# A new order in the attention rounds of a fused attention and expert kernel: query projections behind the keys', ScalarE's copies moved, six early weights split on GpSimd

## Chip, cores and metric

One core of one Trainium2 chip. The metric is device time in microseconds (us), the median of the runs shown; lower is better.

## What is computed

The reference is linear attention with exponential features, and behind it a routed expert layer. Cut to what matters:

```
phi(x):  p = x @ w_phi;  p -= max|p| over the features;  [exp(p), exp(-p)]
kv  = sum over s of phi(k) v          z = sum over s of phi(k)
x   = phi(q) kv / (phi(q) z + 1e-6)   8 batches, 8 heads, 576 tokens, head size 64
e   = argmax(x @ w_gate), or the expert of the token before where local_gate >= 0.5
out = softmax(x @ w_gate)[e] * (relu(x @ w1[e]) @ w2[e])     8 experts, 512 -> 1024 -> 512
```

## The kernel before

**Rounds.** The attention runs in 48 rounds (`round`, line 553) of 384 token positions of a pair of heads, and two more that finish it. Each round works on three generations at once. For its own tokens R it projects the keys into the PSUM tile `pk` and the queries into the PSUM tile `pq` (`proj`, line 326: two banks of 512 columns, two buffers of `pq`), and takes maximum and difference of both on VectorE (`below`, line 335: `mk`, `sbk`, `mq`, `sbq`). For R-1 it turns the query differences into a `pq` tile (`qtr`, line 360), takes their two exponentials on ScalarE (`qexp`, line 366, tile `qp`), and sums keys times values on TensorE (`kv`, `kv4`, tile `kvp`). For an older one it multiplies query features with the summed keys (`num`, line 450) into bank 0 of the tile that held the turned queries; ScalarE copies that to `xo` (line 469) and GpSimd scales it (`scaled`, line 472), sums the gate logits and hands it to a DMA that writes the DRAM array `xs`. There are four buffers of `xo`.

**Summed keys.** When a sum over a batch's keys is complete (two rounds in three), `kv_end` (line 414) copies it to `kvs` on ScalarE (lines 420, 421). The next round turns it: four transposes into columns 384 to 511 of a `pq` tile (line 426), a copy `ks` back on ScalarE (line 433), four small matmuls with the gate weights into the same tile (line 441, "gates"), and a copy of those into `kvs` (line 445). Only then may `num` use `kvs`. Before the change, the four transposes go into the tile of the round before (`past`), into which right behind them the twelve query transposes go (line 572); the queries' projections of the new round follow, into the other buffer.

**What sets the order.** TensorE's order is the order of the code (`manual_schedule`, line 140). The other engines' instructions are placed by a scheduler, held by `issue_after(x)` (not ahead of x on its engine) and `high_priority`. `last_act` and `last_copy` name the last exponential and the last copy on ScalarE. `kv_end` issues its copies behind `last_act`:

```
419  with self.tc.high_priority(), self.tc.issue_after(self.last_act.ins):
420      self.act.copy(kvs[:, :, MID]..., t[:, :, :, 0:D])
421      self.act.copy(kvs[:, :, DEN], t[:, :, :, D])
```

**Background work.** Twice a round `chores` (line 602) takes steps of generators: the routing of a finished batch (`gate`, its reads copied by ScalarE), the scatters of token lists and gathers of tokens by GpSimd's indirect DMAs, each held behind a small copy `tick` (`paced`, line 612), and, when the first two expert slots are planned, the weights of the first of them (`early_weights`, line 523): eight pieces of 128x1024 are loaded into `wraw` (three buffers), and each is split in two halves (`half`, line 544): ScalarE casts to `whi`, GpSimd subtracts to `wlo`.

**Experts.** Behind the rounds the expert slots run (`slots`, line 1408): every product is three float32r matmuls of high and low parts. There ScalarE casts and VectorE subtracts the later weights (`split`, line 1138), one piece at a time as buffers come free. While the first slot runs, the last batch's routing is done on VectorE, with a few small matmuls written into TensorE's order.

Of the kernel before, what the change touches and what calls it, by code (L numbers as in the profile page):

```python
# [7 lines left out]
F32 = mybir.dt.float32  # L8
# [9 lines left out]
B, H, S, D = 8, 8, 576, 64  # L18
# [8 lines left out]
MID, DEN = slice(10, 10 + 2 * D), slice(9, 11 + 2 * D, 2 * D + 1)  # L27
# [4 lines left out]
NR = NBP * NHP * 3  # L32
PLACE = 16
LAG = 1
WE, WR, WL = 8, 3, 2
FILL = 4
ROW = 5
LINE = 256

STEP = "step"  # L40
# [38 lines left out]
class Kernel:  # L79
# [9 lines left out]
    def run(self):  # L89
        nc, tc, A = self.nc, self.tc, self.A  # L90
        act, dve = self.act, self.dve
        with ExitStack() as root:
# [32 lines left out]
            self.tail, self.drained, self.ranked, self.late = False, False, None, 0  # L125
            self.eslots, self.scattered, self.recs = [], [], []
            self.g, self.ch, self.kvb, self.lg, self.kvp, self.summed = {}, {}, {}, {}, {}, {}
            self.f, self.ready, self.scale = {}, {}, []
            self.turns, self.gates, self.background = [], [], []
            self.fetched = 0  # L130
            self.fetch_kq(0)
# [60 lines left out]
            def singles():  # L192
# [4 lines left out]
                       later=[[listed], [no, no, singles] + [lambda k=k: m[k]() for k in (1, 2, 3)] + [more]])  # L197
# [165 lines left out]
            for c in range(3):  # L363
                self.halves(self.f[R]["qt"], (h * 3 + c) * 64, self.f[R]["sq"][:, h, c])

    def qexp(self, R):

        qp = self.f[R]["qp"] = self.feat.tile([128, 2, 2, 384], F32, name="qp")
        src = self.f[R]["qt"][:, :, 0:384].rearrange("p r (a k) -> p a r k", k=64)
        for sg in (0, 1):  # L370
            self.last_copy = self.act.activation(qp[:, sg].rearrange("p h (c r k) -> p (h c) r k", c=3, r=2), src,  # L371
                                                 AF.Exp, scale=1.0 - 2 * sg)

# [40 lines left out]
    def kv_end(self, u, b, t):  # L414


        hp = u % NHP
        kvs = self.back2.tile([128, 2, 2 * (KV + D + 1)], F32, name="kvs", bufs=3)
        with self.tc.high_priority(), self.tc.issue_after(self.last_act.ins):
            self.act.copy(kvs[:, :, MID].rearrange("p s (h d) -> p s h d", h=2), t[:, :, :, 0:D])  # L420
            self.act.copy(kvs[:, :, DEN], t[:, :, :, D])
        e = {}

        def turn(t):
            for sg in (0, 1):
                self.halves(t, 384 + sg * 64, kvs[:, sg, MID])
            self.gates.append(gate)
            return copy

        def copy(t):  # L430
            e["ks"] = self.back2.tile([128, 2, 128], F32, name="ks")
            with self.tc.high_priority():
                self.act.copy(e["ks"].rearrange("p s (r k) -> p s r k", r=2),
                              t[:, :, 384:512].rearrange("p r (s k) -> p s r k", s=2))

        def gate(t):

            g = t[:, 1, 476:512].rearrange("p (s h e) -> p s h e", s=2, h=2)
            for sg in (0, 1):
                for r in (slice(0, 64), slice(64, 128)):  # L440
                    mm = self.last_g = self.pe.matmul(g[r, sg], e["ks"][:, sg, r], self.wgi[:, hp], start=True, stop=True)
                    for x in self.reads:
                        self.tc.declare_no_dep(mm.ins, x.ins, reason="it reads the tile's other bank")
            with self.tc.high_priority(), self.tc.issue_after(self.last_copy.ins):
                self.last_copy = self.act.copy(kvs.rearrange("p s (h x) -> p s h x", h=2)[:, :, :, 0:9], g)  # L445
            self.kvb[u, b] = kvs
            self.ready.update({3 * u + x: 1 for x in ((0,) if b == 0 else (1, 2))})
        self.turns.append(turn)

    def num(self, R, t):  # L450

        u, k = divmod(R, 3)
        bp, hp = divmod(u, NHP)
        c0 = 3 * k
        t = t[:, 0:6 * KV].rearrange("p (c k) -> p c k", c=3)
        qp = self.f[R]["qp"]
        for c in range(3):
            for h in (0, 1):
                k = slice(h * KV, h * KV + KV)
                for sg in (0, 1):  # L460
                    for x in (0, 1):
                        r = slice(64 * x, 64 * x + 64)
                        kvs = self.kvb[u, int(2 * (c0 + c) + x > 8)]
                        self.last_num = self.pe.matmul(t[r, c, k], qp[:, sg, h, c * 128 + 64 * x:c * 128 + 64 * x + 64],  # L464
                                                       kvs[:, sg, k], start=sg == 0, stop=sg == 1)
        del self.f[R]
        xo = self.back2.tile([128, 3, 2 * KV], F32, name="xo", bufs=4)
        with self.tc.high_priority(), self.tc.issue_after(self.last_act.ins):
            self.act.copy(xo, t)
        self.scale.append(lambda: self.scaled(R, bp, hp, c0, xo))  # L470

    def scaled(self, R, bp, hp, c0, xo):
# [35 lines left out]
    def early_chores(self, s, f):  # L508

        w = self.early_weights()  # L510
        for x in f:
            next(w, None)
            yield x
        for x in s:
            for u in range(x["n"]):
                with self.paced():
                    self.gather_x(x, u)
                next(w, None)
                yield STEP
        for _ in w:  # L520
            yield STEP

    def early_weights(self):

        s = self.eslots[0]
        for i in range(min(WE, 8) + LAG):
            if i >= LAG:

                raw, whole = s["raw"].pop(0), self.halved(s)
                self.half(raw, whole, 0)  # L530
            if i < min(WE, 8):
                self.load(s, i)
            yield
            if i >= LAG:
                self.half(raw, whole, 1)
            yield
# [7 lines left out]
    def half(self, raw, whole, k):  # L544

        hi, lo = whole
        c = slice(k * 512, k * 512 + 512)
        with self.tc.issue_after(self.last_act.ins):
            self.act.copy(hi[:, c], raw[:, c])
            for c in (slice(k * 512, k * 512 + 256), slice(k * 512 + 256, k * 512 + 512)):  # L550
                self.pool.tensor_sub(lo[:, c], raw[:, c], hi.bitcast(F32)[:, c])

    def round(self, R):

        new, old = R < NR, 1 <= R <= NR
        if new:
            self.f[R] = {}
            kt = self.psk.tile([128, 2, 512], F32, name="pk")
            self.proj(R, 0, kt)
            sk = self.below(kt, "k")  # L560
        scale, self.scale = self.scale, []
        for x in scale:
            x()
        gates, self.gates = self.gates, []
        turns, self.turns = self.turns, []
        past = self.past_qt if R else None
        copies = [x(past) for x in turns]
        for x in copies:
            x(past)
        gates, self.gates = gates + self.gates, []  # L570
        if old:
            self.qtr(R - 1)
        qt = self.past_qt = self.psq.tile([128, 2, 512], F32, name="pq")
        if new:
            self.f[R]["qt"] = qt
            self.proj(R, 1, qt)
        if old:
            self.qexp(R - 1)
        self.small_ps = [qt[:, 0, 384:512]]
        self.reads = []  # L580
        self.chores()
        mid = 3 * (R - 1) + 1
        if old and mid % NC == 4:
            self.kv4(mid)
        for x in gates:
            x(qt)
        if new:
            self.kexp(R, sk)
            self.f[R]["sq"] = self.below(qt, "q")
        if old:  # L590
            for i in range(3 * (R - 1), 3 * R):
                if i % NC != 4:
                    self.kv(i)
        for k, i in enumerate(sorted(self.ready)[:1 if new else 2]):
            del self.ready[i]
            self.num(i, past[:, 0] if k == 0 else qt[:, 0])
            if not new:
                self.scale.pop()()
        self.small_ps = []
        self.chores()  # L600

    def chores(self):

        for x in list(self.background):
            for _ in range(6):
                y = next(x, self)
                if y is self:
                    self.background.remove(x)
                if y is self or y is STEP:
                    break  # L610
# [958 lines left out]
```

## Time and profile before

| | |
|---|---|
| runs of the kernel | 741.54, 745.0, 744.31 us; median 744.31 |
| the profiled execution | 746.75 us |
| its span, from the first to the last instruction | 744.6 us |
| TensorE busy | 714.7 us, 96% of the span |
| VectorE, ScalarE, GpSimd busy | 421.7, 360.8, 221.5 us |
| granted TensorE clock, mean | 0.994 |

The profile is of one execution; busy time of an engine counts its instructions, not the waits between them. TensorE's weight loads (PEld) run beside its matmuls (PE). A wait is put down to the engine, line and tile that released it last.

### The profile page before, as it was taken

The page shows a single profiled execution, that of the slowest core. Times are in us where ns is not written, and L with a number is a line of the kernel's source. Part 1 is how long each engine was busy: PE and PEld are TensorE (multiplying, and loading weights), DVE is VectorE, ACT ScalarE, POOL GpSimd, SP SyncE. Part 2 cuts the span into 40 slices and gives each one's busy share as a digit, 9 for nine tenths or more (in the row PEclk, how much of TensorE's full clock was granted, in tenths as well). Part 3 has the DMA queues.
Part 4 walks back from the last instruction along what each step waited for, and adds up shares of the span by engine and source line. Part 5 has one row for each costly group of instructions (what it writes and reads, how often), then busy time and mean ns, then how long its engine had stood idle before and what let it go on. Part 6 is the DMA issues. An engine that isn't in the chain of part 4 may idle for free. (4 is left out here: it accounts for less than half of the span.)

```text
span 744.6 us, 22107 instructions
## 1 busy us (share of the span) xinstructions
PE 714.7 (96%) x9448; PEld 623.0 (84%) x9448; DVE 421.7 (57%) x796; ACT 360.8 (48%) x626; POOL 221.5 (30%) x327
## 2 busy tenths in 40 slices
PE   7999999999998989999999999999999999999997
PEld 6888888888888888989888986788878768888985
DVE  6677777677776774584627324544533265453512
ACT  5677767677777866242625224341412055150302
POOL 0322212632377955473232131021212202101011
PEclk9999999999999999999999999999999999999999
DMA  7664454544467761134766984544667364334110
GB/s 228 194 195 131 138 136 130 157 140 130 133 189 217 229 222 38 36 116 132 234 226 198 377 315 149 176 166 155 241 250 282 114 236 170 138 117 160 58 39 29
DMA packets 65540, 125.11 MB, mean 168 GB/s; under 512 B 6908, under 2 KB 44732, under 8 KB 65382
## 3 DMA queue, kind: packets, MB, share of 16 engines
q1 hardware_dynamic: 57152, 100.83, 42.3%
q0 software_dynamic: 7968, 22.58, 8.7%
q8 instruction: 75, 1.23, 0.7%
q10 hardware_dynamic: 320, 0.26, 0.1%
q14 instruction: 25, 0.20, 0.1%
HBM read 102.11 MB, written 21.80 MB: 166 GB/s over the span
## 5 line engine op out<-in xcount | busy, mean ns | idle before, releaser
L1333 ACT ACTIVATE hh<-l 128x512 fp32r<-128x512 f32 (+3 forms) x84 | 44.2, 527 | 196.3 <-PE l L1282 131.7
L1280 PE MATMUL l<-whi,hh 128*128 128x512 f32 (+1 forms) x288 | 114.1, 396 | 0.0
L1334 DVE SCALAR_TENSOR_TENSOR hl<-l,hh 128x512 fp32r<-128x512 f32 (+3 forms) x84 | 50.5, 601 | 112.1 <-ACT hh L1333 111.9
L1150 DVE TENSOR_TENSOR wlo<-wraw,whi 128x1024 fp32r<-128x1024 f32 x80 | 96.5, 1224 | 29.8 <-ACT whi L1147 29.4
L1281 PE MATMUL l<-wlo,hh 128*128 128x512 f32 (+1 forms) x288 | 112.5, 391 | 0.0
L1282 PE MATMUL l<-whi,hl 128*128 128x512 f32 (+1 forms) x288 | 112.4, 390 | 0.0
L1280 PE MATMUL l<-xhi,whi 128*128 128x384 f32 (+4 forms) x308 | 106.8, 347 | 0.0
L1282 PE MATMUL l<-xhi,wlo 128*128 128x384 f32 (+4 forms) x308 | 106.5, 346 | 0.0
L1281 PE MATMUL l<-xlo,whi 128*128 128x384 f32 (+4 forms) x308 | 106.4, 345 | 0.0
L1147 ACT CAST whi<-wraw 128x1024 fp32r<-128x1024 f32 x80 | 81.9, 1046 | 26.9 <-PE l L1282 15.8
L1399 POOL DMA_INDIRECT out<-y,p_tokm x31 | 35.8, 1154 | 190.4 <-DVE y L1393 172.8
L371 ACT ACTIVATE qp<-pq 128x768 f32<-128x768 f32 x96 | 72.6, 808 | 33.3 <-PE pq L358 33.3
L464 PE MATMUL pq<-kvs,qp 128*64 128x74 f32 x2304 | 82.7, 228 | 0.4 <-ACT kvs L445 0.4
L479 POOL TENSOR_TENSOR xo<-xo,rc 128x444 f32<-128x444 f32 x48 | 44.7, 930 | 123.4 <-issue 58.3
L351 ACT ACTIVATE kp<-sbk 128x768 f32<-128x768 f32 x96 | 77.0, 852 | 6.4 <-DVE sbk L342 5.1
L464 PEld LDWEIGHTS pq<-kvs,qp 128*64 128x64 f32 x2304 | 78.1, 137 | 0.5 <-ACT kvs L445 0.5
L386 PE MATMUL kvp<-v,kp 128*64 128x65 f32 x2048 | 72.6, 228 | 0.0
L341 DVE TENSOR_REDUCE mk<-pk 128x6 f32<-128x768 f32 x48 | 45.9, 956 | 46.1 <-PE pk L332 42.1
L386 PEld LDWEIGHTS kvp<-v,kp 128*64 128x64 f32 x2048 | 66.5, 142 | 1.4 <-issue 0.2
L1393 DVE TENSOR_SCALAR y<-l,p_probm 128x512 f32<-128x512 f32 (+1 forms) x31 | 23.2, 749 | 77.0 <-PE l L1282 76.7
L1199 POOL DMA_INDIRECT xg<-xs,p_tokm x32 | 30.9, 965 | 119.3 <-PE tr L1261 101.9
L1282 PEld LDWEIGHTS l<-whi,hl 128*128 128x128 f32 (+1 forms) x288 | 53.2, 185 | 12.4
(266 smaller groups left out, 1189.3 us busy)
## 6 DMA issues: line engine op xcount, KB each, us to landing
wraw<-in_w1h SPq DMA_DIRECT2D x44, 512.0 KB
wraw<-in_w2h SPq DMA_DIRECT2D x44, 512.0 KB
kq<-in_kqT SPq DMA_DIRECT2D x47, 384.0 KB
v<-in_va SPq DMA_DIRECT2D x48, 195.0 KB
xs<-xo SPq DMA_DIRECT2D x48, 192.0 KB
whi<-in_w1h SPq DMA_DIRECT2D x8, 512.0 KB
wlo<-in_w1h SPq DMA_DIRECT2D x8, 512.0 KB
whi<-in_w2h SPq DMA_DIRECT2D x8, 512.0 KB
```

What stands on the lines that cost most here:

```text
L341: dve.tensor_reduce(m, x, AX.X, ALU.max, apply_absolute_value=True)
L351: self.last_act = self.act.activation(kp[:, :, :, sg, :].rearrange("p c h f -> p h c f"), sb, AF.Exp, scale=1.0 - 2 * sg)
L371: self.last_copy = self.act.activation(qp[:, sg].rearrange("p h (c r k) -> p (h c) r k", c=3, r=2), src, AF.Exp, scale=1.0 - 2 * sg)
L386: self.pe.matmul(t[r, sg, h], kp[:, h, sg, r], v[:, h], start=first and sg + h == 0, stop=last and sg + h == 2)
L464: self.last_num = self.pe.matmul(t[r, c, k], qp[:, sg, h, c * 128 + 64 * x:c * 128 + 64 * x + 64], kvs[:, sg, k], start=sg == 0, stop=sg == 1)
L479: pool.tensor_mul(x, x, rc.unsqueeze(3).broadcast_to([128, 3, 2, KV]))
L1147: self.act.copy(hi, raw)
L1150: (low or self.dve).tensor_sub(lo[:, c], raw[:, c], hi.bitcast(F32)[:, c])
L1280: mm(o, ah, bh, start=first, stop=False)
L1281: mm(o, ah, bl, start=False, stop=False)
L1282: self.last_pe = mm(o, al, bh, start=False, stop=last)
L1334: self.marks[dve] = dve.scalar_tensor_tensor(hl[:, hc, m], t, 0.0, hh[:, hc, m].bitcast(F32), ALU.max, ALU.subtract)
```

## The change

Five edits. The queries' projections stand right behind the keys'. The summed keys are turned into the new round's `pq` tile, and only the query transposes go into the round's before, their own. The first query exponential stands ahead of the gates, the second behind their copy. The `kvs` copies are put behind the round's `xo` copy (a list `later`), and `xo` becomes `last_act`. The early weights are six in place of eight, their casts are GpSimd's, and they take a step once a round in place of twice.

```diff
+EW = 6
@@ qexp
-    def qexp(self, R):
+    def qexp(self, R, sg):
+        if sg == 0:
+            self.f[R]["qp"] = self.feat.tile([128, 2, 2, 384], F32, name="qp")
-        for sg in (0, 1):
+        with self.tc.issue_after(self.last_copy.ins) if sg else nullcontext():
             self.last_copy = self.act.activation(...)
@@ kv_end
+        def fetch():
+            with self.tc.high_priority(), self.tc.issue_after(self.last_act.ins):
                 ...
+        if self.past_qt is self.f.get(NR - 1, {}).get("qt") or max(self.f) < NR - 1:
+            self.later.append(fetch)
+        else:
+            fetch()
@@ num
-            self.act.copy(xo, t)
+            self.last_act = self.act.copy(xo, t)
@@ early_chores, early_weights
         for x in f:
-            next(w, None)
+            if not self.second:
+                next(w, None)
...
-        for i in range(min(WE, 8) + LAG):
+        for i in range(EW + LAG):
@@ half
-        with self.tc.issue_after(self.last_act.ins):
-            self.act.copy(hi[:, c], raw[:, c])
-            for c in (slice(k * 512, k * 512 + 256), slice(k * 512 + 256, k * 512 + 512)):
-                self.pool.tensor_sub(lo[:, c], raw[:, c], hi.bitcast(F32)[:, c])
+        self.pool.tensor_copy(hi[:, c], raw[:, c])
+        for c in (slice(k * 512, k * 512 + 256), slice(k * 512 + 256, k * 512 + 512)):
+            self.pool.tensor_sub(lo[:, c], raw[:, c], hi.bitcast(F32)[:, c])
@@ round
+        past = self.past_qt if R else None
+        qt = self.past_qt = self.psq.tile([128, 2, 512], F32, name="pq")
         if new:
             self.proj(R, 0, kt)
             sk = self.below(kt, "k")
...
+        if new:
+            self.proj(R, 1, qt)
-        copies = [x(past) for x in turns]
-        for x in copies:
-            x(past)
+        for x in [x(qt) for x in turns]:
+            x(qt)
         if old:
             self.qtr(R - 1)
-        qt = self.past_qt = self.psq.tile([128, 2, 512], F32, name="pq")
-        if new:
-            self.proj(R, 1, qt)
-        if old:
-            self.qexp(R - 1)
+            self.qexp(R - 1, 0)
...
         for x in gates:
             x(qt)
+        if old:
+            self.qexp(R - 1, 1)
...
+        later, self.later = self.later, []
+        for x in later:
+            x()
-        self.small_ps = []
+        self.small_ps, self.second = [], True
         self.chores()
+        self.second = False
```

TensorE in a turned round, one early in the rounds; before (`pq<-first,kvs` are the turns, `pq<-first,sbq` the query transposes, line 441 the gates, line 464 `num`):

```order
L332 MATMUL pk<-first,kq 128x128 x6
L358 MATMUL pq<-first,kvs 128x64 x4
L358 MATMUL pq<-first,sbq 128x64 x12
L332 MATMUL pq<-first,kq 128x128 x6
L441 MATMUL pq<-wgi,ks 64x18 x4
L386 MATMUL kvp<-v,kp 64x65 x24
L464 MATMUL pq<-kvs,qp 64x74 x24
```

The same round after the change:

```order
L333 MATMUL pk<-first,kq 128x128 x6
L333 MATMUL pq<-first,kq 128x128 x6
L359 MATMUL pq<-first,kvs 128x64 x4
L359 MATMUL pq<-first,sbq 128x64 x12
L450 MATMUL pq<-wgi,ks 64x18 x4
L389 MATMUL kvp<-v,kp 64x65 x24
L473 MATMUL pq<-kvs,qp 64x74 x24
```

The queries' six projections moved ahead of the turns; the query transposes now stand directly ahead of the gates, between the turns and the readers of `ks`.

ScalarE in a turned round, from one `xo` to the last copy ahead of the next; before (the first `kvs` is the gates' copy, the two behind `kp` fetch the next sum):

```order
L469 COPY xo<-pq 128x444
L433 COPY ks<-pq 128x256
L371 ACTIVATE qp<-pq 128x768 x2
L445 COPY kvs<-pq 128x4x9
L351 ACTIVATE kp<-sbk 128x2x3x128 x2
L420 COPY kvs<-kvp 128x2x128
L421 COPY kvs<-kvp 128x2x2
```

After:

```order
L478 COPY xo<-pq 128x444
L425 COPY kvs<-kvp 128x2x128
L426 COPY kvs<-kvp 128x2x2
L442 COPY ks<-pq 128x256
L374 ACTIVATE qp<-pq 128x768
L454 COPY kvs<-pq 128x4x9
L374 ACTIVATE qp<-pq 128x768
L352 ACTIVATE kp<-sbk 128x2x3x128 x2
```

The two fetching copies moved from ahead of `xo` to behind it, and the gates' copy stands between the two exponentials of the queries.

GpSimd where the first early weight is split; before (line 551 subtracts, 479 is the product of `xo`, 811 a scatter):

```order
L618 COPY tick<-mq 128x1
L811 DMA lst<-pr,ri 36992x16
L551 TENSOR_TENSOR wlo<-wraw,whi 128x256 x4
L618 COPY tick<-mk 128x1
L811 DMA lst<-pr,ri 36992x16
L479 TENSOR_TENSOR xo<-xo,rc 128x444
L486 TENSOR_TENSOR lg<-lg,xo 128x27
```

After (line 561 is the cast, 563 subtracts, 488 is the product, 825 a scatter):

```order
L632 COPY tick<-mk 128x1
L825 DMA lst<-pr,ri 36992x16
L561 CAST whi<-wraw 128x512 x2
L488 TENSOR_TENSOR xo<-xo,rc 128x444
L563 TENSOR_TENSOR wlo<-wraw,whi 128x256
L495 TENSOR_TENSOR lg<-lg,xo 128x27
L563 TENSOR_TENSOR wlo<-wraw,whi 128x256
L496 TENSOR_TENSOR lg<-lg,xo 128x27
L563 TENSOR_TENSOR wlo<-wraw,whi 128x256 x2
```

The casts now stand in GpSimd's queue ahead of the product of `xo`, and the subtractions between its sums.

## Rows read from the trace of the kernel before

**Rows 1.** The page, part 1: busy us, share and instructions of each engine

```profile
PE 714.7 (96%) x9448; PEld 623.0 (84%) x9448; DVE 421.7 (57%) x796; ACT 360.8 (48%) x626; POOL 221.5 (30%) x327
```

**Rows 2.** Waits of TensorE and its weight loader: us in total, times, longest

```profile
PE pq L358 <- ACT ks L433: 13.9, 30, 0.5
PE pq L358 <- DVE sbq L342: 1.4, 5, 0.6
...
PEld pq L358 <- ACT ks L433: 18.0, 30, 0.6
```

**Rows 3.** Timeline, a turned round: start, us, engine, line, operation, count [idle before]

```profile
87.40 0.94 PE L332 MATMUL pk<-first,kq 64*128 64x128 f32 x12
87.56 0.53 ACT L469 COPY xo<-pq 128x444 f32<-128x444 f32 x1 [0.37 <-DMA kq<-in_kqT]
...
88.17 0.29 PE L358 MATMUL pq<-first,kvs 64*128 64x64 f32 x4
...
88.49 0.37 ACT L433 COPY ks<-pq 128x256 f32<-128x256 f32 x1 [0.40 <-PE pq L358]
...
88.92 0.59 PE L358 MATMUL pq<-first,sbq 64*128 64x64 f32 x12 [0.46 <-ACT ks L433]
...
89.34 0.89 PE L332 MATMUL pq<-first,kq 64*128 64x128 f32 x12
...
89.54 1.51 ACT L371 ACTIVATE qp<-pq 128x768 f32<-128x768 f32 x2 [0.68 <-PE pq L358]
...
90.16 0.41 PE L441 MATMUL pq<-wgi,ks 128*64 128x18 f32 x8
...
90.41 1.60 PE L386 MATMUL kvp<-v,kp 128*64 128x65 f32 x48
...
91.01 1.60 ACT L351 ACTIVATE kp<-sbk 128x768 f32<-128x768 f32 x2
...
91.84 1.71 PE L464 MATMUL pq<-kvs,qp 128*64 128x74 f32 x48
...
93.48 0.94 PE L332 MATMUL pk<-first,kq 64*128 64x128 f32 x12
```

**Rows 4.** Timeline, the plain round ahead of it

```profile
82.19 0.94 PE L332 MATMUL pk<-first,kq 64*128 64x128 f32 x12
...
82.96 0.53 PE L358 MATMUL pq<-first,sbq 64*128 64x64 f32 x12
...
83.53 1.51 ACT L371 ACTIVATE qp<-pq 128x768 f32<-128x768 f32 x2 [0.65 <-PE pq L358]
...
84.15 0.70 PE L399 MATMUL kvp<-v,kp 64*64 64x65 f32 x32
...
85.75 1.71 PE L464 MATMUL pq<-kvs,qp 128*64 128x74 f32 x48
```

**Rows 5.** Busy time by stretch: PE, PEld, DVE, ACT, POOL, PEclk, DMA, GB/s

```profile
234.00:238.00 4.00, 4.00 (x79) 3.88 (x79) 2.70 (x4) 3.79 (x8) 2.86 (x7) 0.57 0.34 82
```

**Rows 6.** Timeline of TensorE, the two longest waits among the early weights

```profile
232.10 0.34 PE L358 MATMUL pq<-first,kvs 64*128 64x64 f32 x4 [1.01 <-ACT kvs L421]
...
267.26 0.94 PE L332 MATMUL pq<-first,kq 64*128 64x128 f32 x12 [1.38 <-ACT xo L469]
```

**Rows 7.** Groups by line, GpSimd: count | busy us, mean ns | idle before

```profile
L479 POOL TENSOR_TENSOR xo<-xo,rc 128x444 f32<-128x444 f32 x48 | 44.7, 930 | 123.4 <-issue 58.3 <-ACT qp L371 35.8 <-ACT kvs L445 9.5
L811 POOL DMA_INDIRECT lst<-pr,ri x36 | 36.9, 1026 | 14.4 <-DVE ri L75 7.4 <-issue 5.4
...
L551 POOL TENSOR_TENSOR wlo<-wraw,whi 128x256 fp32r<-128x256 f32 x32 | 22.3, 730 | 4.0 <-ACT whi L549 3.9
L486 POOL TENSOR_TENSOR lg<-lg,xo 128x27 f32<-128x27 f32 x36 | 8.7, 242 | 2.8
...
L618 POOL COPY tick<-mq 128x1 f32<-128x1 f32 x21 | 4.0, 191 | 22.5 <-DVE mq L341 22.5
```

**Rows 8.** Groups by line, VectorE: the splits of later weights

```profile
L1150 DVE TENSOR_TENSOR wlo<-wraw,whi 128x1024 fp32r<-128x1024 f32 x80 | 96.5, 1224 | 29.8 <-ACT whi L1147 29.4
```

More of the change, by code (lines that the diff above doesn't have):

```diff
@@ L127, in run @@
             self.g, self.ch, self.kvb, self.lg, self.kvp, self.summed = {}, {}, {}, {}, {}, {}
-            self.f, self.ready, self.scale = {}, {}, []
+            self.f, self.ready, self.scale, self.later, self.second = {}, {}, [], [], False
             self.turns, self.gates, self.background = [], [], []
@@ L364, in qtr @@
                 self.halves(self.f[R]["qt"], (h * 3 + c) * 64, self.f[R]["sq"][:, h, c])
-    def qexp(self, R):
-        qp = self.f[R]["qp"] = self.feat.tile([128, 2, 2, 384], F32, name="qp")
+    def qexp(self, R, sg):
+        if sg == 0:
+            self.f[R]["qp"] = self.feat.tile([128, 2, 2, 384], F32, name="qp")
+        qp = self.f[R]["qp"]
         src = self.f[R]["qt"][:, :, 0:384].rearrange("p r (a k) -> p a r k", k=64)
-        for sg in (0, 1):
+        with self.tc.issue_after(self.last_copy.ins) if sg else nullcontext():
             self.last_copy = self.act.activation(qp[:, sg].rearrange("p h (c r k) -> p (h c) r k", c=3, r=2), src,
@@ L418, in kv_end @@
         kvs = self.back2.tile([128, 2, 2 * (KV + D + 1)], F32, name="kvs", bufs=3)
-        with self.tc.high_priority(), self.tc.issue_after(self.last_act.ins):
-            self.act.copy(kvs[:, :, MID].rearrange("p s (h d) -> p s h d", h=2), t[:, :, :, 0:D])
-            self.act.copy(kvs[:, :, DEN], t[:, :, :, D])
+        def fetch():
+            with self.tc.high_priority(), self.tc.issue_after(self.last_act.ins):
+                self.act.copy(kvs[:, :, MID].rearrange("p s (h d) -> p s h d", h=2), t[:, :, :, 0:D])
+                self.act.copy(kvs[:, :, DEN], t[:, :, :, D])
+        if self.past_qt is self.f.get(NR - 1, {}).get("qt") or max(self.f) < NR - 1:
+            self.later.append(fetch)
+        else:
+            fetch()
         e = {}
@@ L517, in early_chores @@
                     self.gather_x(x, u)
-                next(w, None)
+                if not self.second:
+                    next(w, None)
                 yield STEP
@@ L521, in early_chores @@
             yield STEP
+            while self.second:
+                yield STEP
     def early_weights(self):
         s = self.eslots[0]
-        for i in range(min(WE, 8) + LAG):
+        for i in range(EW + LAG):
             if i >= LAG:
@@ L530, in early_weights @@
                 self.half(raw, whole, 0)
-            if i < min(WE, 8):
+            if i < EW:
                 self.load(s, i)
@@ L547, in half @@
         c = slice(k * 512, k * 512 + 512)
-        with self.tc.issue_after(self.last_act.ins):
-            self.act.copy(hi[:, c], raw[:, c])
-            for c in (slice(k * 512, k * 512 + 256), slice(k * 512 + 256, k * 512 + 512)):
-                self.pool.tensor_sub(lo[:, c], raw[:, c], hi.bitcast(F32)[:, c])
+        self.pool.tensor_copy(hi[:, c], raw[:, c])
+        for c in (slice(k * 512, k * 512 + 256), slice(k * 512 + 256, k * 512 + 512)):
+            self.pool.tensor_sub(lo[:, c], raw[:, c], hi.bitcast(F32)[:, c])
     def round(self, R):
         new, old = R < NR, 1 <= R <= NR
+        past = self.past_qt if R else None
+        qt = self.past_qt = self.psq.tile([128, 2, 512], F32, name="pq")
         if new:
-            self.f[R] = {}
+            self.f[R] = {"qt": qt}
             kt = self.psk.tile([128, 2, 512], F32, name="pk")
@@ L563, in round @@
             x()
-        gates, self.gates = self.gates, []
+        if new:
+            self.proj(R, 1, qt)
         turns, self.turns = self.turns, []
-        past = self.past_qt if R else None
-        copies = [x(past) for x in turns]
-        for x in copies:
-            x(past)
-        gates, self.gates = gates + self.gates, []
+        for x in [x(qt) for x in turns]:
+            x(qt)
         if old:
             self.qtr(R - 1)
-        qt = self.past_qt = self.psq.tile([128, 2, 512], F32, name="pq")
-        if new:
-            self.f[R]["qt"] = qt
-            self.proj(R, 1, qt)
-        if old:
-            self.qexp(R - 1)
+            self.qexp(R - 1, 0)
         self.small_ps = [qt[:, 0, 384:512]]
@@ L584, in round @@
             self.kv4(mid)
+        gates, self.gates = self.gates, []
         for x in gates:
             x(qt)
+        if old:
+            self.qexp(R - 1, 1)
         if new:
```

## The prediction

> **What bounds the kernel now.** I read the page's busy shares first. TensorE is busy 714.7 of 744.6 us [rows 1]: what an edit can win is either TensorE's 30 us of idle time, or time in which TensorE works slowly. The waits of TensorE say where the idle time is: 30 times, 0.46 us each, the transposes of the queries (line 358) wait for ScalarE's copy `ks` [rows 2]. The weight loader shows the same wait as 18.0 us, 0.60 each, since its work can't run ahead either. All this lies in the 48 rounds before 302 us; behind them TensorE shows no wait worth naming, so a gain there is kept to the end.
>
> Then one round of each kind on the timeline. In a *turned* round [rows 3] (summed keys are turned: two rounds in three) the reader is to see 6.08 us from one `pk` to the next (87.40 to 93.48), and in it 0.75 us between the four turns (88.17) and the queries' transposes (88.92), which is ScalarE's copy there and back. A *plain* round [rows 4] takes 5.21 us (82.19 to 87.40) and has no such hole. Last, the stretch in which the early weights are split: TensorE stands still 1.01 us for `kvs` and 1.38 us for `xo` [rows 6], both behind a cast of weights in ScalarE's queue, and some us after each the granted clock is 0.57 over 4 us (one of the two stretches stands in [rows 5]; the other, 268 to 272, reads 0.57 as well), so partly at the lower of its levels, 1.2 of 2.4 GHz.
>
> **The turned round, step by step.** All offsets are from the start of `pk`. Before: turns +0.77, copy `ks` +1.09 to +1.46, queries' transposes +1.52, `pq` +1.94, gates +2.76, `kvp` +3.01, `num` +4.44, end +6.08 [rows 3]. The change puts `pq` behind `pk`. Its buffer is the one that the last `num` wrote and `xo` reads; `xo` runs from +0.16 to +0.69, and a releaser's end reaches TensorE 0.06 us later (`ks` ends 88.86, transposes 88.92). So `pq` starts about +0.82 in place of +0.77, and as it takes 0.82 the turns start at +1.64. The two small `kvs` copies now stand behind `xo`, and have until the turns to end: in time. `ks` again starts 0.32 behind the turns (+1.96) and ends +2.33; the gates, its readers, can start 0.75 behind the turns, +2.39. But the twelve query transposes now lie inside this hole (+1.77 to +2.16), so of 0.75 us only some 0.25 stay empty. `kvp` follows 0.25 after the gates, `num` 1.43 after that: +4.07. `num` writes the tile that both exponentials `qp` read; they start 0.6 behind the transposes (+2.37), take 1.51 with the gates' small copy between them, and end near +4.0: no wait yet. The end is at +5.71: **0.37 us less, 30 times, 11.1 us.**
>
> **The plain round.** `pq` +0.82, transposes +1.64, `kvp` +2.01; `num` would come 1.60 later (84.15 to 85.75 [rows 4]) at +3.61. But `qp` starts 0.57 behind the transposes, +2.21, and ends at +3.72, so `num` waits to +3.78. The end is +5.42 in place of 5.21: **0.21 us more, 15 times, 3.2 us.** This is a new wait that the change makes. Both results have ends: if `pq` and `num` wait for nothing, a turned round loses 0.42 and a plain one nothing, 12.6 us together; if every ScalarE step is 0.15 us late, a turned round wins 0.2 and a plain one costs 0.4, which is nothing together. I take **7.9 us**.
>
> **ScalarE's queue.** In the new order `kp` stands behind the second `qp` (near +3.9 in a turned round) and takes 1.60 [rows 3]: it ends near +5.5, and the next `xo` is wanted 0.16 after the round's end, at +5.87. That is 0.4 us of cover; in a plain round it is +3.7 and 1.60 against 5.42 and 0.16, some 0.3. Everything queued behind a late `kp` is `xo`, and behind `xo` now stands TensorE itself.
>
> **The early weights.** The casts of these weights leave ScalarE, and with them the two stalls above; the last two of eight weights move to the first expert slot. The stalls are 2.4 us; the slow clock behind them costs 2 x 4 x (1 - 0.57) = 3.4 us. A stall goes only if its cause does: ScalarE now waits for no weight, since only GpSimd does, and the loads lie two rounds ahead of the casts. I take **6 us**, between 2.4 (the clock falls anyway) and 8.
>
> GpSimd pays: from the first cast to the last, 11 rounds or some 62 us, it has 11 `xo` products of 0.93 with two sums of 0.24 each, 12 indirect DMAs of 1.03 with a tick of 0.19 each, and 24 subtractions of 0.73 [rows 7]: 48 us, and the 12 casts. No row shows a GpSimd cast of 128x512. Below, it can't be under the 0.2 of a tick; above, two subtractions of 128x256 are 1.46. It is nearer to the upper, being the same columns with one operand less: I take 1.0, which makes 60 of 62 us. So GpSimd is full but not late; for the times that ScalarE waits for a buffer of `xo` I put **1 us**, from 0 to 4. The Trainium skill (GPSIMD Engine Reference, sections 3.1 and 4.1) speaks against this edit: it keeps elementwise work off GpSimd, and gives 768 ns for 512 elements of one input. By that figure the sum would be an estimated 57 of 62 us, and the 1 us would go; what the rows allow is wider, so I keep their bounds.
>
> **The rest.** Five times, 1.4 us, the turns or transposes wait for VectorE's `sbq` [rows 2]; they now come 0.82 us later: **1.4 us** gone. In the first expert slot two splits of 1.22 us [rows 8] come onto VectorE ahead of the copy that feeds the last gate, whose matmuls stand in TensorE's order; its slack I can't read to better than some tenths: **0.4 us** more, from 0 to 1.2. ScalarE's two casts there lie between activations for which it waits anyhow. SP's queue loses two loads in the rounds and gets them back at the slot's start, with writes of `xs` behind them that nobody reads in that slot: nothing, and 1 us if that cover is gone.
>
> **Sum:** -7.9 - 6 + 1 - 1.4 + 0.4 = -13.9 us. The profiled execution took 746.75 us, 2.1 over its span, and stands 2.4 above the median of the three runs, 744.31. 746.75 - 13.9 = 732.9; less 2.4, **730 us**.
>
> **Rivals.** *All waits hidden:* `pq` and `num` wait for nothing and the weights' stretch loses 8: -12.6 - 8 - 1.4 = -22, 722 us. For it: ScalarE shows idle time in every round; against it: `xo` can't end before +0.69. Chance 0.17.
>
> *The hole only moves:* the gates wait for `ks` as long as the transposes did, as the refill of TensorE's pipeline (0.60 against 0.46 [rows 2]) is paid in either place, and the plain rounds still pay. Then -0.1 x 30 + 3.2 - 6 + 1 - 1.4 + 0.4, some -6, which is 738; with the clock falling as before, 742. This is the case in which the change does not do what it says. Against it: the transposes are 0.42 us of work that needs nothing of `ks`. Chance 0.13.
>
> *GpSimd becomes the bound (slower):* if a cast takes c, GpSimd needs 48 + 12c in 62 us. Beyond c = 1.2 it falls behind; with four `xo` buffers it may lag by three rounds, some 17 us, before ScalarE's `xo`, and so TensorE's `pq`, wait for it. To cancel the 14 us c must reach 1.2 + (17 + 14) / 12 = 3.8 us; at 4.2 the time is some 749. For it: the sum above leaves GpSimd 2 us in 62; against it: 0.73 for half the columns with two operands. The rule of that page of the Trainium skill is this mechanism, though its own figure would not bring it about. A second way to the same place is ScalarE's cover of 0.3 to 0.4 us: an extra 0.7 us on ScalarE in every round would cost 0.35 x 45 = 16 us. Chance together 0.06.
>
> **How the numbers follow.** The forecast has 0.64. A measurement of this kernel can tell about 0.5%, 3.7 us, from no change, so faster is below 740.6. Faster: forecast, all hidden, and four tenths of the moved hole: 0.64 + 0.17 + 0.05 = 0.86; the rest of that hole is no change, 0.08; slower 0.06. The range takes the forecast's bounds (12.6 or 0 for the rounds, 8 or 2.4 for the weights, 0 or 4 for GpSimd, not all at one end at once) and both faster rivals: 720 to 740.
>
> **What would show it.** Right: no wait of line 359 on `ks`; a wait of the gates on `ks` of some 0.2 us, 30 times; a small wait of `pq` on `xo` in nearly every round; `num` on `qp` in plain rounds; rounds of 5.7 and 5.4 us; clock 1.0 throughout the weights. Wrong: `xo` late by more than 0.2 us in most rounds (ScalarE bounds), GpSimd without idle time and ScalarE waiting for it, casts over 1.5 us, or TensorE idle at the first expert slot.

## The result and the profile after

| | before | after |
|---|---|---|
| median of the runs compared | 744.57 us (4 runs) | 733.00 us (4 runs) |
| ratio | | 0.985, 95% interval 0.983 to 0.988 |
| profiled execution, and its span | 746.75, 744.6 | 732.99, 731.1 |
| start of round 0 to start of round 47 | 281.84 | 266.06 |
| start of round 47 to the end of the span | 459.15 | 460.95 |

Forecast 730 us, between 720 and 740; it took 733. The page, part 1, against [rows 1]: TensorE has lost 6 us of busy time and 7 of idle time.

```profile
PE 708.6 (97%) x9448; PEld 621.9 (85%) x9448; DVE 419.2 (57%) x798; ACT 354.3 (48%) x612; POOL 222.5 (30%) x331
```

The waits of TensorE and its weight loader (us in total, times, longest), against [rows 2]: the 30 waits of the transposes for `ks` are gone. In their place the weight loader waits for `ks` 20 times, 0.2 us each, at the gates (line 450). New are two waits of 2.3 us, and one of 1.3 that the trace puts down to nothing.

```profile
PE pk L333 <- DMA first<-in_first: 4.1, 1, 4.1
PE pq L333 <- ACT xo L478: 2.3, 1, 2.3
PE pq L922 <- DMA lr<-lst,p_rie: 2.3, 1, 2.3
...
PE pq L333 <- issue: 1.6, 2, 1.3
...
PE pq L359 <- ACT xo L478: 0.7, 1, 0.7
...
PEld pq L450 <- ACT ks L442: 4.6, 20, 0.2
```

The timeline of a turned round, against [rows 3] (start, us, engine, line, operation, count [idle before]). It is 5.59 us long, and every matmul stands right behind the one before it but for some 0.2 us ahead of the gates. `pq` comes 0.77 behind `pk`, without a wait for `xo`, and takes 0.75.

```profile
84.12 0.94 PE L333 MATMUL pk<-first,kq 64*128 64x128 f32 x12
...
84.89 0.91 PE L333 MATMUL pq<-first,kq 64*128 64x128 f32 x12
...
85.64 0.28 PE L359 MATMUL pq<-first,kvs 64*128 64x64 f32 x4
85.75 0.54 PE L359 MATMUL pq<-first,sbq 64*128 64x64 f32 x12
85.96 0.37 ACT L442 COPY ks<-pq 128x256 f32<-128x256 f32 x1 [0.67 <-PE pq L359]
...
86.39 0.41 PE L450 MATMUL pq<-wgi,ks 128*64 128x18 f32 x8
86.64 1.60 PE L389 MATMUL kvp<-v,kp 128*64 128x65 f32 x48
87.04 0.19 ACT L454 COPY kvs<-pq 128x36 f32<-128x36 f32 x1
...
88.07 1.71 PE L473 MATMUL pq<-kvs,qp 128*64 128x74 f32 x48
89.71 0.38 PE L333 MATMUL pk<-first,kq 64*128 64x128 f32 x2
```

A plain round, against [rows 4]: 5.35 us to the next `pk` at 67.60, `num` at +3.66 where it was at +3.56. It starts 0.06 behind the end of `qp` (64.34 + 1.51 = 65.85); so short a wait is not marked in the view.

```profile
62.25 0.94 PE L333 MATMUL pk<-first,kq 64*128 64x128 f32 x12
...
64.34 1.51 ACT L374 ACTIVATE qp<-pq 128x768 f32<-128x768 f32 x2 [1.40 <-PE pq L359]
...
65.91 1.76 PE L473 MATMUL pq<-kvs,qp 128*64 128x74 f32 x48
```

Among the early weights the two stalls of [rows 6] are gone, but rounds 40 and 41 take 8.44 and 7.97 us. In their timeline GpSimd is to be followed first: its cast of the second weight (line 561) stands 3.63 us for the load of that weight, and what is queued behind it stands too. Its list read (line 891) is issued only at 223.68, so TensorE waits 2.26 for the list (line 922). Its last gate sum (line 496) ends at 229.35, behind three subtractions of weights; VectorE has stood 6.42 us at `g_mx`, which reads it, and everything queued behind `g_mx` is late: `mk`, with it `kp` on ScalarE, behind that `xo`, and at the end of the chain TensorE's `pq`, 2.29 us.

```profile
221.29 1.17 POOL L561 CAST whi<-wraw 128x512 fp32r<-128x512 f32 x2 [3.63 <-DMA wraw<-in_w1h]
...
223.68 0.95 POOL L891 DMA_INDIRECT lr<-lst,p_rie  x1 [0.19 <-issue]
...
225.75 2.08 POOL L563 TENSOR_TENSOR wlo<-wraw,whi 128x256 fp32r<-128x256 f32 x3
...
227.84 0.35 PE L922 MATMUL pq<-first,lr 6*128 6x6 f32 x2 [2.26 <-DMA lr<-lst,p_rie]
...
229.11 0.24 POOL L496 TENSOR_TENSOR lg<-lg,xo 128x27 f32<-128x27 f32 x1
229.38 0.23 DVE L76 TENSOR_REDUCE g_mx<-lg 128x9 f32<-128x72 f32 x1 [6.42 <-POOL lg L496]
...
235.07 0.94 PE L333 MATMUL pq<-first,kq 64*128 64x128 f32 x12 [2.29 <-ACT xo L478]
```

The casts wait so for all six weights, 16.9 us together (the waits of GpSimd, columns as above):

```profile
POOL whi L561 <- DMA wraw<-in_w1h: 10.7, 4, 3.6
POOL whi L561 <- DMA wraw<-in_w2h: 6.2, 2, 5.0
```

Busy time by stretch (columns as in [rows 5]): TensorE is idle for 1.8 of 4 us in one stretch and for 1.1 in another, and the granted clock stays at 1.00.

```profile
226.00:230.00 4.00, 2.17 (x65) 2.18 (x67) 0.58 (x3) 1.56 (x5) 3.19 (x6) 1.00 0.44 130
...
234.00:238.00 4.00, 2.93 (x85) 2.67 (x87) 3.08 (x9) 2.26 (x6) 2.57 (x5) 1.00 0.84 255
```

### The profile page after: what moved, and what is told of

Same layout as the page of the kernel before. It is cut to its first block, busy times and chain, and to the rows that moved or that the text cites. A ratio compares the mean times of both kernels' runs of the same rounds, so it can differ in the third digit from the quotient of the medians.

```text
span 731.1 us, 22070 instructions
## 1 busy us (share of the span) xinstructions
PE 708.6 (97%) x9448; PEld 621.9 (85%) x9448; DVE 419.2 (57%) x798; ACT 354.3 (48%) x612; POOL 222.5 (30%) x331
## 5 line engine op out<-in xcount | busy, mean ns | idle before, releaser
L1164 DVE TENSOR_TENSOR wlo<-wraw,whi 128x1024 fp32r<-128x1024 f32 x82 | 99.0, 1223 | 30.7 <-ACT whi L1161 29.9
L1161 ACT CAST whi<-wraw 128x1024 fp32r<-128x1024 f32 x82 | 84.0, 1046 | 27.9 <-PE l L1296 15.9
L374 ACT ACTIVATE qp<-pq 128x768 f32<-128x768 f32 x96 | 76.3, 815 | 25.6 <-PE pq L359 25.6
L389 PE MATMUL kvp<-v,kp 128*64 128x65 f32 x2048 | 70.7, 223 | 0.0
L389 PEld LDWEIGHTS kvp<-v,kp 128*64 128x64 f32 x2048 | 64.5, 138 | 1.5 <-issue 0.2
```

Of the source, the lines that this page charges most:

```text
L389: self.pe.matmul(t[r, sg, h], kp[:, h, sg, r], v[:, h], start=first and sg + h == 0, stop=last and sg + h == 2)
L1161: self.act.copy(hi, raw)
L1164: (low or self.dve).tensor_sub(lo[:, c], raw[:, c], hi.bitcast(F32)[:, c])
```

## The experiments

Each kernel ran beside the kernel before on the same chip; the ratio is to that. The three times are read from the starts of `pk` in each trace: a turned round, the ten rounds 37 to 46 (the early weights), and what follows round 47's start.

| kernel | ratio, 95% interval | turned | 37 to 46 | rest |
|---|---|---|---|---|
| before | 1 | 6.09 | 67.50 | 459.15 |
| after | 0.985 (0.983 to 0.988) | 5.59 | 63.27 | 460.95 |
| change_again | 0.984 (0.982 to 0.987) | 5.59 | 64.28 | 460.71 |
| turns_past | 1.012 (1.010 to 1.013) | 6.24 | 65.41 | 467.64 |
| pq_late | 1.003 (1.001 to 1.005) | 6.21 | 64.75 | 461.28 |
| one_exp | 0.984 (0.982 to 0.986) | 5.59 | 60.42 | 462.36 |
| order_only_2 | 0.984 (0.981 to 0.986) | 5.59 | 63.35 | 460.71 |
| weights_only_2 | 1.011 (1.009 to 1.014) | 6.09 | 67.12 | 466.84 |
| kvs_at_once_2 | 0.991 (0.989 to 0.993) | 5.59 | 61.94 | 467.62 |
| pool_behind | 0.976 (0.974 to 0.978) | 5.59 | 57.74 | 460.67 |
| behind_eight | 0.977 (0.975 to 0.980) | 5.59 | 56.89 | 462.76 |

The theory at the start: the rounds' gain is TensorE's order alone, and GpSimd's split of the early weights gives back what it saves, because GpSimd's queue holds up the list and the gates' sums. The rivals: the split is worth its 5 us, or ScalarE's order carries the gain.

### The order without the weights, the weights without the order

order_only, from the changed kernel:

```diff
-EW = 6
+EW = 8
@@ half
-        self.pool.tensor_copy(hi[:, c], raw[:, c])
+        with self.tc.issue_after(self.last_act.ins):
+            self.act.copy(hi[:, c], raw[:, c])
@@ round
-        self.small_ps, self.second = [], True
+        self.small_ps, self.second = [], False
```

> The changed kernel with the early weights split as before: ScalarE casts, eight tiles, twice a round. Theory (the gain is TensorE's new order; GpSimd's split gives back what it saves, because its queue holds back the list read and the gates' sums): 732 to 735 us, within 0.3% of the changed kernel, ScalarE's late copies back among the early weights, the waits on GpSimd gone. Rival (moving the split is worth the 5 us of the forecast on its own): 737 to 739 us.

weights_only is the opposite: the kernel before with `EW = 6`, the cast on GpSimd, and `second`.

> The kernel before with only the split of the early weights changed: GpSimd casts, six tiles, once a round. Theory: 742 to 745 us, within 0.4% of the kernel before, since the waits of 1.0 and 1.4 us and the stretch at a clock of 0.57 go but waits on GpSimd's sums and on the list come. Rival (the split is a gain of its own): 738 to 740 us.

The first measured 743.1 us, 0.993 (0.991 to 0.994), above both ranges; the second 755.9, 1.011 (1.009 to 1.013), slower than either expectation. But in order_only rounds 22, 25, 34 and 36 took 7.1 to 7.3 us, and rounds 21 to 36 together 8.6 us more than in the changed kernel; the first early weight is split in round 37. The run couldn't decide between 0.993 and the changed kernel's 0.985. So both were run again, and the changed kernel too:

> The changed kernel once more, beside the others on one chip. Expected: a ratio of 0.983 to 0.988 against the kernel before, as in the first comparison. If the rounds in which GpSimd scatters the list are longer here, as they were with the order alone (7.25 us where 5.59 is the rule), the ratio is 0.990 to 0.995, and the split of the early weights has not been shown to be worth anything.

> The changed kernel with the early weights split as before (ScalarE, eight tiles, twice a round), once more: in the first run its rounds from the 22nd on were 1.1 to 1.7 us longer than the same rounds of the changed kernel on another chip, long before the first early weight, so its total told nothing of the weights. Theory (the split as changed gives back what it saves): rounds 22 to 38 as in the changed kernel (5.6 and 5.3 us), 731 to 736 us, 0.981 to 0.988 of the kernel before. Rival (the split is worth 5 us as forecast): 737 to 739 us, 0.990 to 0.993.

> The kernel before with only the split of the early weights changed, once more, for the same reason. In the first run rounds 40 and 42 took 9.4 and 11.9 us and the round of 8.9 and that of 9.2 us were gone. Theory: GpSimd's late sums cost more than the ScalarE casts did, 1.002 to 1.008 of the kernel before. Rival (the split is a gain of its own): 0.990 to 0.995.

On two other chips change_again came to 732.9 and order_only_2 to 731.95 us, and no round of theirs from 22 to 36 is over 5.8: the theory holds for the weights. With ScalarE's casts rounds 37 to 46 take 63.35 us, with GpSimd's 63.27 and 64.28, so **the split as changed is worth nothing measurable**. Alone in the old order it costs 1.1%, on both chips; more than the 0.2 to 0.8% expected. The waits of TensorE in weights_only_2 say where (columns as above; its line 913 is the list's transposes, 1329 the first expert product, 470 `xo`):

```profile
PE l L1329 <- ACT xo L470: 5.5, 1, 5.5
PE pq L913 <- DMA lr<-lst,p_rie: 4.8, 1, 4.8
```

The list read is late by 4.8 us, and a wait of 5.5 stands behind round 47. There too GpSimd's casts wait for all six loads, 28.5 us together. After the first of them the clock is down, which the busy time by stretch shows (columns as in [rows 5]); in the changed kernel it was not:

```profile
240.00:244.00 4.00, 1.52 (x24) 1.50 (x26) 2.10 (x4) 0.42 (x3) 1.61 (x4) 0.50 0.50 118
```

### The two halves of the new order

turns_past puts the turned sums back into the tile of the round before; pq_late keeps them in the new tile and puts the queries' projections back behind the turned queries:

```diff
@@ turns_past, round
-        for x in [x(qt) for x in turns]:
-            x(qt)
+        for x in [x(past) for x in turns]:
+            x(past)
@@ pq_late, round
-        if new:
-            self.proj(R, 1, qt)
         turns, self.turns = self.turns, []
...
             self.qtr(R - 1)
+        if new:
+            self.proj(R, 1, qt)
+        if old:
             self.qexp(R - 1, 0)
```

> The changed kernel with the turned sums back in the tile of the round before, all else as changed. Theory (in a turned round the copy xo out of that tile ends about 0.7 us after the round's start and the queries' projections end at 1.5 us, so the turns find the tile free either way; the order alone fills the hole): 732 to 735 us. Rival (the tile is what took the wait away): the turns wait again, 0.3 to 0.5 us in 30 rounds, 742 to 748 us.

> The changed kernel with the queries' projections put back behind the turned queries; the turned sums stay beside this round's queries. Putting them in the tile of the round before made a turned round 6.24 us where it is 5.59, so the tile is needed. Theory (the order is needed as well: the turns write the tile that xo empties until 0.7 us after the round's start and read kvs, whose copies end at 1.2 us, and without the projections ahead nothing covers that): TensorE waits 0.4 to 0.7 us in a turned round, 30 times, 12 to 20 us more than the changed kernel. Rival (the tile alone is the gain): within 0.3% of the changed kernel.

turns_past took 757.8 us: the expectation fell. The rival had the direction, but not the size, nor the instruction that waits: a turned round got 0.65 us longer and the rest 6.9, and it is not the turns that wait but the queries' transposes. Its timeline, a turned round from 87.02 (columns as above), shows it: they go into the same tile as the turns, and wait until ScalarE has read `ks` out of it, wherever the projections stand.

```profile
88.86 0.37 ACT L442 COPY ks<-pq 128x256 f32<-128x256 f32 x1 [0.68 <-PE pq L359]
89.28 0.59 PE L359 MATMUL pq<-first,sbq 64*128 64x64 f32 x12 [0.47 <-ACT ks L442]
```

pq_late took 746.8 us, 14 more than change_again, as expected. Here the transposes follow the turns at once, but the turns themselves are late: they wait for the second copy `kvs`, which stands behind `xo`, and come at +1.21 in place of +0.77 (the round starts at 86.54). Then `pq` comes 0.63 behind the transposes, where its weight loads wait 0.23 for `ks`. Its plain rounds are back at 5.21 us.

```profile
87.75 0.34 PE L359 MATMUL pq<-first,kvs 64*128 64x64 f32 x4 [0.27 <-ACT kvs L426]
87.92 0.54 PE L359 MATMUL pq<-first,sbq 64*128 64x64 f32 x12
```

So neither half alone shortens a turned round of this kernel: 6.24 and 6.21 us, against 6.09 before. **The tile takes the wait for `ks` off the transposes; the projections cover the copies `kvs`, which the change has put behind `xo`.** That the projections would be needed with those copies in their old place is not shown. In kvs_at_once_2 (below) they stand ahead of `xo`; the second ends 0.16 into the round (88.68), `xo` at 0.70, and the turns could start at 0.77:

```profile
88.51 0.17 ACT L426 COPY kvs<-kvp 128x4 f32<-128x4 f32 x1
88.52 0.94 PE L333 MATMUL pk<-first,kq 64*128 64x128 f32 x12
88.69 0.53 ACT L478 COPY xo<-pq 128x444 f32<-128x444 f32 x1
```

With the copies there pq_late could save the 0.44 us by which its turns are late: by these rows an estimated 5.77 us for a turned round, more than half of the gain. No run has the tile alone with the copies in their old place.

### ScalarE's order

one_exp puts both exponentials of the queries ahead of the gates' copy; kvs_at_once issues the copies `kvs` at once and lets nothing wait for `xo`:

```diff
@@ one_exp, round
             self.qexp(R - 1, 0)
+            self.qexp(R - 1, 1)
...
-        if old:
-            self.qexp(R - 1, 1)
@@ kvs_at_once, kv_end and num
-        if self.past_qt is self.f.get(NR - 1, {}).get("qt") or max(self.f) < NR - 1:
-            self.later.append(fetch)
-        else:
-            fetch()
+        fetch()
...
-            self.last_act = self.act.copy(xo, t)
+            self.act.copy(xo, t)
```

> The changed kernel with both exponentials of the queries ahead of the gates' copy on ScalarE. The gates' copy ends 0.84 us before the numerators that read it, and an exponential of 0.83 us put ahead of it eats just that. Theory: 0 to 0.2 us in each of 30 turned rounds, 0 to 0.8% above the changed kernel. Rival (the split of the exponentials is a large part of the gain): over 0.4 us in a turned round, 1.5% or more above the changed kernel.

> The changed kernel with the copies kvs issued at once again, ahead of the copy xo on ScalarE, and nothing held behind xo. Theory (the queries' projections need the tile that xo empties, and the copy ends only about 0.1 us before they start): with two copies of together 0.6 us ahead of it, TensorE waits some 0.5 us in the rounds that have one, 30 times, 742 to 750 us. Rival (ScalarE's order of these is covered): 732 to 736 us.

> The changed kernel with the copies kvs issued at once, once more on a chip without the long rounds. In the first run its clean rounds were those of the changed kernel (5.59 and 5.35 us), so the expectation of 742 to 750 us has fallen for them. Theory now (ScalarE's order of kvs and xo is covered): 730 to 735 us, 0.981 to 0.988 of the kernel before. Rival (it costs where rounds are late already): 0.990 or more.

one_exp took 731.55 us, no difference in the total; its rounds 37 to 46 are 3.9 us shorter than change_again's, its rest 1.65 longer. In its timeline the gates' copy ends at 88.05 and the numerators that read it start at 88.19, as far into the round (3.95 us) as in the changed kernel: the cover of 0.84 us was just enough.

```profile
87.85 0.20 ACT L454 COPY kvs<-pq 128x36 f32<-128x36 f32 x1
...
88.19 1.71 PE L473 MATMUL pq<-kvs,qp 128*64 128x74 f32 x48
```

kvs_at_once first took 744.5 us, 0.995 (0.994 to 0.997), within the expected range but not for the expected reason: four rounds again took 7.2 to 7.3. The second run took 737.7. Its turned and plain rounds are those of the changed kernel, so the expectation of 0.5 us in 30 rounds fell; but 5 us are lost, as the rival had it, and not on ScalarE. Round 40 takes 11.70 us, of which 3.7 are a wait for the list, but rounds 37 to 46 together are 1.3 to 2.3 shorter than in the changed kernel's two traces. The loss is all behind round 47, 6.7 to 6.9 us. There subtractions and three paced scatters stand in GpSimd's queue ahead of a product on an `xo` that was copied at 278.37; ScalarE's `xo` waits 6.75 us for a buffer, and the first expert product behind it 6.40. Its timeline, columns as above:

```profile
285.29 0.98 POOL L825 DMA_INDIRECT lst<-pr,ri  x1 [0.16 <-issue]
286.28 0.95 POOL L488 TENSOR_TENSOR xo<-xo,rc 128x444 f32<-128x444 f32 x1
...
289.45 0.53 ACT L478 COPY xo<-pq 128x444 f32<-128x444 f32 x1 [6.75 <-POOL lg L496]
290.03 1.65 PE L1338 MATMUL l<-xhi,whi 128*128 128x384 f32 x4 [6.40 <-ACT xo L478]
```

An edit of ScalarE's order alone had changed the order that the scheduler gives GpSimd, and by the trace the loss comes from there. Neither of these two edits changes a turned round; both together were not run.

### GpSimd's queue: a version that beats both

pool_behind holds the split behind the round's own sums, and changes nothing else; TensorE's order is the same, row for row:

```diff
@@ half
-        self.pool.tensor_copy(hi[:, c], raw[:, c])
-        for c in (slice(k * 512, k * 512 + 256), slice(k * 512 + 256, k * 512 + 512)):
-            self.pool.tensor_sub(lo[:, c], raw[:, c], hi.bitcast(F32)[:, c])
+        with self.tc.issue_after(self.last_pool.ins):
+            self.pool.tensor_copy(hi[:, c], raw[:, c])
+            for c in (slice(k * 512, k * 512 + 256), slice(k * 512 + 256, k * 512 + 512)):
+                self.pool.tensor_sub(lo[:, c], raw[:, c], hi.bitcast(F32)[:, c])
```

> The changed kernel with GpSimd's split of the early weights held behind the round's own sums in its queue. Theory (the split ahead of the sums delays the gates' sums and the list read, which TensorE then waits 2.3 us each for): the rounds of 8.4 and 8.0 us shorten, 3 to 5 us less than the changed kernel. Rival (the waits there have another cause, or the split is then late for the first expert): within 0.2% of the changed kernel or above.

It took 725.9 us beside change_again's 732.9 on the same chip: 7 us less, where 3 to 5 were expected, 0.976 of the kernel before. Rounds 40 and 41 take 5.91 and 5.48 us. Its timeline, columns as above: the list read is out at 216.41, and the last sum ends at 222.51, ahead of the cast; `g_mx` stood 0.76 us. None of the six waits of casts for loads is left.

```profile
216.41 0.92 POOL L891 DMA_INDIRECT lr<-lst,p_rie  x1 [0.94 <-DVE sbq L343]
...
222.27 0.24 POOL L496 TENSOR_TENSOR lg<-lg,xo 128x27 f32<-128x27 f32 x1
...
222.54 0.23 DVE L76 TENSOR_REDUCE g_mx<-lg 128x9 f32<-128x72 f32 x1 [0.76 <-POOL lg L496]
```

So the order of GpSimd's queue cost the 7 us. The hold does two things at once: the sums go ahead of the split, and a cast no longer stands at the head of the queue before its load has landed. No run takes these apart.

Two tiles more, `EW = 8` on top of it, asked whether the missing tiles are what makes the rest longer:

> GpSimd's split held behind the round's sums, and eight early tiles instead of six. With six, the stretch from the last round's start to the end was 460.7 to 461.0 us against 459.2 in the kernel before, which split eight. Theory (two tiles too few for the first expert cost that 1.5 us): 724 to 726 us, 0.971 to 0.976 of the kernel before. Rival (the two more tiles hold up GpSimd's last scatter, on which the other experts' list hangs): 727 to 732 us.

It took 727.35 us, and its interval overlaps that of pool_behind. The rest is 2.1 us longer with eight tiles, not 1.5 shorter, and order_only_2 had eight as well with 460.71: the number of tiles isn't what lengthens the rest. Nor is it GpSimd's last scatter: TensorE waits 1.75 us for the last batch's routing, `g_code`. From the start of `g_mx`, VectorE's chain to it takes 3.24 us here and 1.48 in pool_behind, because some of its small instructions are stretched while GpSimd splits the two tiles. First behind_eight, then the same instructions in pool_behind:

```profile
284.91 2.79 POOL L563 TENSOR_TENSOR wlo<-wraw,whi 128x256 fp32r<-128x256 f32 x4
284.95 0.78 DVE L76 TENSOR_TENSOR g_eq<-g_eq,consts 128x72 f32<-128x72 f32 x1
...
286.38 0.65 DVE L76 TENSOR_TENSOR g_code<-g_code,g_rs 128x9 f32<-128x9 f32 x1
...
287.09 0.28 PE L727 MATMUL pt<-first,g_code 128*9 128x128 f32 x1 [1.75 <-DVE g_code L76]
```

```profile
284.03 0.22 DVE L76 TENSOR_TENSOR g_eq<-g_eq,consts 128x72 f32<-128x72 f32 x1
...
284.79 0.16 DVE L76 TENSOR_TENSOR g_code<-g_code,g_rs 128x9 f32<-128x9 f32 x1
```

## Why the prediction came out right

The total was right by luck: two of its terms were wrong in opposite directions, the rounds by 5 us and the early weights by 4.

- **The rounds: mechanism right, undersized.** The hole was filled by the query transposes, as forecast; the gates kept a wait of 0.2 us, forecast 0.25. A turned round lost 0.50 us, not 0.37, and a plain one got 0.14 longer, not 0.21: 30 x 0.50 - 15 x 0.14 = 12.9 us, where I took 7.9 and gave 12.6 as the end. The failed step is "`pq` starts about +0.82 ... and as it takes 0.82 the turns start at +1.64". The wait for `xo` didn't exist: `pq` starts when `pk` is through, at +0.77, and takes 0.75. By the prediction's own rows `xo` ends at +0.69 and its release reaches TensorE 0.06 later, at +0.75, ahead of that; the +0.82 was a wrong sum. So the turns, and with them the gates, `num` and the end of a turned round, come 0.12 us earlier than forecast. Of the two small waits listed as signs, `pq` on `xo` is absent. `num` on `qp` is there in the plain rounds, as forecast: `num` comes 0.06 behind the end of `qp`, and 0.10 later in the round than before. That the tile is needed besides the order wasn't in the forecast; turns_past shows it.
- **VectorE's `sbq`: right.** Those five waits are gone. They were 0.16 us in round 1, 0.20 in 18 and 30, and 0.56 and 0.25 in rounds 42 and 44, among the early weights.
- **The early weights: wrong.** I took -6 and +1 for GpSimd. Rounds 37 to 46 lost 4.2 us, of which 7 turned and 3 plain rounds are 3.1 by themselves; 1.1 are left (0.1 in change_again), and order_only_2 shows that even these need no GpSimd cast. Two steps failed, "the loads lie two rounds ahead of the casts" and "So GpSimd is full but not late". The loads lie less than a round ahead: that of the second weight is issued at 216.9, and its cast waits until 221.29, at the head of the queue. A cast took 0.61 us, not 1.0, so by the prediction's sum GpSimd's work is 48 + 12 x 0.61 = 55 of 62 us. The Trainium skill (GPSIMD Engine Reference, section 3.1) gives 768 ns as the best case for 512 elements; this trace's 0.61 us is below it. GpSimd's work left room, and yet it was late, because of what stood ahead of what in its queue: the 16.9 us for which casts waited for loads were in no sum. I had summed its work and read neither its order nor its waits. With the order mended, pool_behind's ten rounds take 57.74: 67.50 - 3.1 - 57.74 = 6.7 us. Of these 0.8 are the waits for `sbq` in rounds 42 and 44, and 5.9 are left, so the 6 us of stalls and slow clock were there to be had.
- **Start and rest: undersized.** Forecast +0.4; the rest came out 1.8 longer, and the start, TensorE's first wait for a load, 0.5. The 1.8 is not the first expert slot, where I had put the 0.4: its first product starts 17.95 us behind round 47's start, where it was 16.14, and from there both kernels take 443.0 us. It is lost in the last rounds. There 0.67 is read on the waits: without projections, nothing stands between the turns and `xo` (line 359). The other 1.1 isn't settled.
- **The rivals.** *The hole only moves* didn't happen: the gates' wait is 0.2 us. In turns_past the hole stays where it was, ahead of the transposes. *GpSimd becomes the bound* fell by its price, since a cast took 0.61 and not 3.8, but its way (GpSimd late, a buffer of `xo` held, TensorE waiting) is how weights_only became 1.1% slower and kvs_at_once lost 5 us.

Accounts of the profiled executions: -15.8 in the rounds, +0.5 and +1.8 at the ends, -13.5 in span; forecast -13.9. For the profiled execution the forecast was 732.9 us, and it took 732.99. The 3 us between 730 and the median of 733 are the 2.4 taken off because the profile of the kernel before lay above its median, and that of the changed kernel doesn't. Between the medians the change is worth 11.6 us.

## What to carry to other kernels

When work is moved to an engine with an in-order queue, a sum of its busy time says little: list what stands in the queue ahead of each result that another engine waits for, and what each of these waits for itself, and pin that order. A hole behind a copy out of a tile can be closed by another tile for what needn't wait and independent work ahead of what must; try the parts singly, and leave the rest of the order as it was for each, or a part will be misjudged. A gain that a scheduler decides elsewhere (here GpSimd's order after an edit of ScalarE's) can hide that of the edit, so compare equal rounds before totals.

## What was not expected of the hardware

**VectorE stretched beside GpSimd.** In round 43 of the changed kernel a cast of 9x128 on VectorE took 1.64 us, where the instruction of its size just before it took 0.21, and TensorE waited 0.73 for it. It ended 0.08 us behind GpSimd's product (line 488):

```profile
246.64 1.64 DVE L76 CAST g_ef<-g_ci 9x128 f32<-9x128 int32 x1
247.26 0.94 POOL L488 TENSOR_TENSOR xo<-xo,rc 128x444 f32<-128x444 f32 x1
...
248.43 0.20 PE L756 MATMUL pq<-first,g_ef 9*128 9x9 f32 x1 [0.73 <-DVE g_ef L76]
```

The Trainium skill (SBUF — State Buffer, section "Who interferes with whom") says that a cast on VectorE can contend with a GpSimd instruction for a shared pair of ports, and that the loser blocks until the other is done. Where the cast ended agrees with it; that it starts 0.62 us ahead of that product is not explained by it. The nearest to a test are the rows of behind_eight and pool_behind above: the same VectorE instructions took 0.78 and 0.65 us beside GpSimd's subtractions, 0.22 and 0.16 beside its scatters, while the reductions between them took 0.22 to 0.23 in both.

**The clock after a wait.** In the changed kernel waits of 2.26 and 2.29 us left the granted clock at 1.00, while in the kernel before waits of 1.01 and 1.38 us were followed by 0.57 [rows 5, 6], and in weights_only_2 one of 4.8 us by 0.50. The length of the wait alone doesn't tell what follows.

**Idle time without a releaser.** In order_only's round 22 ScalarE's `xo` started 0.9 us later than in other rounds, with nothing in the trace that it waited for:

```profile
122.92 0.53 ACT L478 COPY xo<-pq 128x444 f32<-128x444 f32 x1 [1.36 <-issue]
```

Such rounds came in all four kernels of one chip, where GpSimd scatters the list, and in no kernel on the other chips there; single ones came elsewhere (rounds 9 and 10 of the changed kernel, 0.36 and 0.63 us). Their cause stays open.
